# Fixed order on all DMA queues, a hand-pipelined first phase and weights paced in half tiles, in an attention and mixer kernel

## The chip, the cores and the metric

The kernel runs on one core of a Trainium2 chip. The metric is the device time of one execution in microseconds (us). Engines are named as in the profile: PE (TensorE: matmuls and weight loads), DVE (VectorE), ACT (ScalarE), POOL (GpSimd) and SP (SyncE, which here only issues DMAs). Each of SP and POOL has a queue of its own from which it issues DMAs in order.

## The reference

The input x has 2048 tokens of 1024 features, in bf16. Two branches read the normalised x. Branch A is attention over segments of 32 tokens with a memory of 8 rows that each segment hands to the next; branch B is a mixer with an MLP. Their sum and x make the output.

```python
# A: 32 heads of 128, 64 segments of 32 tokens
h = concatenate([mem, xs])                  # 8 memory rows + 32 tokens
q, k, v = h @ Wq, h @ Wk, h @ Wv
p = softmax(where(mask, q @ k.T * scale, -1e9))
o = (p @ v) @ Wo
mem = o[:8]                                 # for the next segment
out_A = o[8:]
# B
h = gelu(layernorm(x) @ w1)                 # 1024 -> 1024
hs = shifted quarters of h @ w2             # shifts of 1 and 2 tokens
x1 = x + hs
out_B = x1 + gelu(layernorm(x1) @ w3) @ w4  # 1024 -> 3584 -> 1024
```

## The kernel before

The serial chain of memories is not followed. The kernel computes, with sums over each segment, what the memories are if softmax is close to uniform over a segment ("speculative" units), runs the attention of all segments in parallel with them, and at the end compares the memories it got with those it assumed. A fallback that goes segment by segment stands behind a condition and isn't run here.

The order of PE's instructions is the order of the program text (`manual_schedule` with PE alone, line 186). On DVE, ACT, POOL and SP a scheduler chooses the order. Every engine takes its own instructions strictly in its order, so an instruction that waits holds up all behind it.

The stages, one after another on PE:

1. *First phase* (L202 to L301). Sixteen tiles of 128 tokens. For each, `norm` takes statistics on DVE (L222 to L227), two inverse square roots on POOL (L229), minus mean times root on DVE (nm2, L231), the branch-B normalisation `xn2` on ACT (L233), the branch-A normalisation `xn` on DVE (L237), and stores `xn` to a scratch in DRAM by POOL's queue (L238). For tiles 0 to 3 `xn2` is transposed by PE (L247), for tiles 4 to 15 by a DMA transpose on SP (L235). `stage1` multiplies by w1 (L264) and applies gelu (L266); `seg_sums` (L256) makes the sums over segments. Groups have 1, 1, 2, 2, 2, 4 and 4 tiles. w2 comes as one load of 2 MB (L298). w3's seven loads of 1 MB (L335) stand later in the text, but the scheduler lets them run in this phase.
2. *The w2 phase* (L306 to L329). For each tile the w2 matmuls (L315), the reload of `xn` from the scratch (L308), an add on DVE (L316) and statistics (L317), the root on POOL (L323), nm3 on DVE (L325), `xn3` on ACT (L327), the store of x1 (R1) by POOL's queue (L328) and a DMA transpose to `xn3T` on SP (L329).
3. *The MLP* (L432 to L466), four blocks of 512 tokens. A block has 28 groups of w3 matmuls (L436) with gelu (L437), and then for each of its four tiles loads of R1 and x (L453, L455), an add on POOL (L456), 56 w4 matmuls (L460), adds on DVE (L461) and the store of R (L466). Between them run 24 speculative units. Each loads 1 MB of Wv or Wo by SP (L364, L376, L398) into a pool of four weight slots and later multiplies it by a few columns (L370, L384, L404). `spec_step` runs one unit and loads the next. In the last block sixteen DMA transposes make `xT` from the scratch.
4. *The V phase* (L472 to L490). Eight loads of Wv (L475), 1024 matmuls (L481), evictions on ACT and DVE, stores of V (L486).
5. *Attention* (L607 to L671), five groups of tokens, eight groups of four heads in each. A group of heads loads 1 MB of Wq and of Wk (L629, L630) and its V (L524), and projects (L540). Scores of a tile (L551) go through DVE (L553), ACT's exp (L555), and DVE again (L557, L559, L563) to `Pn`, which a DMA transpose on SP (L566) turns into `PT` for the output matmuls (L575). `tick` places scores and outputs between projections by a clock estimated in the program; outputs come LAT = 8 estimated us after their scores. Wo comes in four loads of 2 MB in the first group (L637). At the third group of heads `block_setup` makes the transposed tokens of the next group, `hTb`, with four DMA transposes (L515) and four small DVE copies (L516). After a group its output matmuls (L593) run, with a load of R (L596), an add (L601) and the store of the result (L602) at the last of eight pieces.
6. *The end*: the comparison of the memories and the last output pieces.

Of the kernel before, what the change touches and what calls it, by code (L numbers as in the profile page):

```python
# [15 lines left out]
BF16 = mybir.dt.bfloat16  # L16
# [7 lines left out]
P = 128  # L24
# [6 lines left out]
H = 32  # L31
# [46 lines left out]
def kernel(  # L78
# [107 lines left out]
    with tc.manual_schedule(engines={mybir.EngineType.PE}), ExitStack() as actx:  # L186
# [5 lines left out]
        with ExitStack() as bctx:  # L192
            psum = bctx.enter_context(tc.tile_pool(name="psum", bufs=2, space=PSUM))
            with ExitStack() as hctx:
# [4 lines left out]
                nc.gpsimd.memset(hTB[:, :, 0:2], 0.0)  # L199
                nc.gpsimd.memset(hTB[:, :, S + 2:S + 4], 0.0)  # L200

                with ExitStack() as p0:  # L202
# [3 lines left out]
                    xts = [ring.tile([P, D], BF16, tag="xt", bufs=8, name=f"xt{n}") for n in range(NT)]  # L206

                    def load_x(n):
                        nc.sync.dma_start(xts[n][:], x_v[:, n, :])
# [5 lines left out]
                    for n in range(3, 8):  # L215
                        load_x(n)

                    def norm(n, xn2T, jj, on_pe):
                        xt = xts[n]
                        st = ring.tile([P, 2, 6], F32, tag="st")  # L220
                        for c in range(2):
                            nc.vector.bn_stats(st[:, c, :], xt[:, c * 512:(c + 1) * 512])  # L222
                        mv = ring.tile([P, 2], F32, tag="mv")
                        nc.vector.bn_aggr(mv[:], st[:])
                        ab = ring.tile([P, 2], F32, tag="ab")
                        nc.vector.tensor_scalar(ab[:, 0:1], mv[:, 1:2], EPS, None, op0=ALU.add)
                        nc.vector.tensor_scalar(ab[:, 1:2], ab[:, 0:1], EPS, mv[:, 1:2], op0=ALU.mult, op1=ALU.add)  # L227
                        rr = ring.tile([P, 2], F32, tag="rr")
                        nc.gpsimd.tensor_tensor(rr[:], ab[:], neghalf[:], op=ALU.pow)  # L229
                        nm2 = ring.tile([P, 1], F32, tag="nm2")  # L230
                        nc.vector.tensor_scalar(nm2[:], mv[:, 0:1], rr[:, 1:2], -1.0, op0=ALU.mult, op1=ALU.mult)  # L231
                        xn2 = ring.tile([P, D], BF16, tag="xn2")
                        nc.scalar.activation(xn2[:], xt[:], ACTF.Identity, bias=nm2[:], scale=rr[:, 1:2])  # L233
                        if not on_pe:
                            nc.sync.dma_start_transpose(xn2T[:, jj], xn2[:])  # L235
                        xn = ring.tile([P, D], BF16, tag="xn")
                        nc.vector.tensor_scalar(xn[:], xt[:], mv[:, 0:1], rr[:, 0:1], op0=ALU.subtract, op1=ALU.mult)  # L237
                        nc.gpsimd.dma_start(xn_v[:, n, :], xn[:])  # L238
                        if n + 8 < NT:
                            load_x(n + 8)  # L240
                        return xn, xn2

                    def transposes(xn2, xn2T, jj):
                        for k0 in (0, 4):
                            ps = psum0.tile([P, 4, P], F32, tag="tr")
                            for k in range(4):
                                nc.tensor.matmul(ps[:, k, :], xn2[:, (k0 + k) * P:(k0 + k + 1) * P], ident[:], start=True, stop=True)  # L247
                            if k0 == 0:
                                nc.vector.tensor_copy(xn2T[:, jj, k0:k0 + 4, :], ps[:])
                            else:  # L250
                                nc.scalar.copy(xn2T[:, jj, k0:k0 + 4, :], ps[:])

                    def seg_sums(n, xn):
# [3 lines left out]
                        nc.vector.tensor_copy(xsum[:, :, 4 * n:4 * n + 4], ps[:])  # L257

                    def stage1(n0, nt, xn2T, between):
                        w = nt * P  # L260
                        for co in range(KT):
# [5 lines left out]
                            if between and co % 2 == 1:  # L267
                                between.pop(0)()

                    groups = []  # L270
                    n0 = 0
                    for nt in (1, 1, 2, 2, 2, 4, 4):
                        groups.append((n0, nt))
                        n0 += nt
                    todo = []
                    prev = None
                    for (n0, nt) in groups:
                        xn2T = ring.tile([P, 4, KT, P], BF16, tag="xn2T", bufs=2)
                        on_pe = n0 < 4
                        trs, sms = [], []  # L280
                        for jj in range(nt):
                            xn, xn2 = norm(n0 + jj, xn2T, jj, on_pe)
                            if on_pe:
                                trs.append(lambda xn2=xn2, jj=jj, xn2T=xn2T: transposes(xn2, xn2T, jj))
                            sms.append(lambda n=n0 + jj, xn=xn: seg_sums(n, xn))
                        if prev is None:
                            for f in trs:
                                f()
                            todo = sms
                        else:  # L290
                            todo = trs + todo
                            stage1(*prev, todo)
                            for f in todo:
                                f()
                            todo = sms
                        prev = (n0, nt, xn2T)
                        if n0 == 4:
                            nc.sync.dma_start(w2_sb[:], w2_v)  # L298
# [554 lines left out]
```

## Time and profile before

| | |
|---|---|
| median of 3 runs | 1609.46 us (1600.1 to 1611.64) |
| the profiled execution | 1606.37 us |
| its span | 1604.6 us |
| mean granted PE clock | 0.988 |
| PE busy | 1537.0 us (96%) |
| DVE, ACT, POOL busy | 525.3, 511.5, 89.7 us |
| read from and written to DRAM | 191.52 and 42.53 MB |

The profile is of one execution. Its own time is 1.8 us more than the span, which runs from the first instruction to the last event. PE is busy nearly all the time, so time is to be found where PE waits. A wait on another engine counts only if PE, or the end of the program, comes to wait for it.

### The profile page before, as it was taken

The page shows a single profiled execution, that of the slowest core. Times are in us where ns is not written, and L with a number is a line of the kernel's source. Part 1 is how long each engine was busy: PE and PEld are TensorE (multiplying, and loading weights), DVE is VectorE, ACT ScalarE, POOL GpSimd, SP SyncE. Part 2 cuts the span into 40 slices and gives each one's busy share as a digit, 9 for nine tenths or more (in the row PEclk, how much of TensorE's full clock was granted, in tenths as well). Part 3 has the DMA queues.
Part 4 walks back from the last instruction along what each step waited for, and adds up shares of the span by engine and source line. Part 5 has one row for each costly group of instructions (what it writes and reads, how often), then busy time and mean ns, then how long its engine had stood idle before and what let it go on. Part 6 is the DMA issues. An engine that isn't in the chain of part 4 may idle for free.

```text
span 1604.6 us, 25081 instructions
## 1 busy us (share of the span) xinstructions
PE 1537.0 (96%) x10222; PEld 830.5 (52%) x10222; DVE 525.3 (33%) x1149; ACT 511.5 (32%) x1183; POOL 89.7 (6%) x114
## 2 busy tenths in 40 slices
PE   5799998999999999999999999999999999999998
PEld 4544444454454444444455645654655566466654
DVE  6248000001010112212235533551554165325541
ACT  4423300301202101111146623650563266146630
POOL 4223001001011010000000000000000000000000
PEclk9899999999999999999999999999999999999999
DMA  9869525265382567433369965993798388348521
GB/s 316 242 190 298 190 86 177 79 208 186 91 243 75 109 193 266 132 105 120 105 196 254 236 155 131 245 232 89 213 233 201 108 223 228 91 128 196 115 48 48
DMA packets 340087, 271.93 MB, mean 169 GB/s; under 512 B 155987, under 2 KB 309736, under 8 KB 339968
## 3 DMA queue, kind: packets, MB, share of 16 engines
q1 hardware_dynamic: 333888, 249.23, 58.2%
q0 software_dynamic: 6080, 21.05, 3.5%
q8 instruction: 82, 1.34, 0.4%
q14 instruction: 37, 0.30, 0.1%
HBM read 191.52 MB, written 42.53 MB: 146 GB/s over the span
## 4 chain that ended last, share of the span: by engine, by line
PE 73%; DMA 9%; DVE 1%; issue 1%; ACT 0%; POOL 0%; SPq 0%; ACTq 0%; POOLq 0%
PE ps L540 23%; PE pso L593 14%; PE ps L481 14%; PE ps L436 9%; PE ps L460 8%; DMA PT<-Pn_6360 3%; PE psO L575 2%; PE psS L551 2%; DMA PT<-Pn_6361 2%; DMA PT<-Pn_6359 1%; DMA hTb<-xn_scratch 1%; PE ps L693 1%; DMA R_scratch<-R_3128 1%; PE ps L404 1%; DMA wot<-in_A_Wo_dram 1%
## 5 line engine op out<-in xcount | busy, mean ns | idle before, releaser
L540 PE MATMUL ps<-hTb,wt 128*128 128x396 bf16 (+1 forms) x2560 | 403.7, 311 | 0.0
L540 PEld LDWEIGHTS <-wt 128*128 128x128 bf16 x3072 | 272.0, 98 | 167.3 <-issue 4.5
L481 PE MATMUL ps<-wt,xT 128*128 128x512 bf16 x1024 | 221.2, 379 | 0.0
L460 PE MATMUL ps<-w_sb,h3T 128*128 128x512 bf16 x896 | 198.5, 382 | 0.0
L437 ACT ACTIVATE h3T<-ps 128x512 bf16<-128x512 f32 x112 | 66.6, 597 | 315.0 <-PE ps L436 310.6
L481 PEld LDWEIGHTS <-xT 128*128 128x128 bf16 x1024 | 100.2, 98 | 120.8
L436 PEld LDWEIGHTS <-w_sb 128*128 128x128 bf16 x896 | 88.1, 99 | 112.3 <-issue 11.4
L460 PEld LDWEIGHTS <-h3T 128*128 128x128 bf16 x896 | 87.1, 98 | 103.3 <-issue 2.7
L557 DVE TENSOR_REDUCE sums<-sm 99x4 f32<-99x396 f32 (+1 forms) x176 | 97.6, 554 | 117.6 <-ACT sm L555 117.5
L553 DVE TENSOR_TENSOR sm<-psS,c_mask_reg_sb 99x396 f32<-99x396 f32 x160 | 91.2, 570 | 109.6 <-PE psS L551 108.9
L483 ACT CAST Vs<-ps 128x512 bf16<-128x512 f32 x64 | 37.4, 586 | 230.2 <-PE ps L481 177.5
L555 ACT ACTIVATE sm<-sm 99x396 f32<-99x396 f32 (+1 forms) x176 | 92.8, 527 | 54.0 <-DVE sm L553 49.8
L485 DVE CAST Vs<-ps 128x512 bf16<-128x512 f32 x64 | 44.3, 692 | 176.5 <-PE ps L481 172.7
L540 PE MATMUL ps<-hTb_5138,wt 128*128 128x403 bf16 x512 | 93.6, 335 | 2.4 <-ACT QT_6369 L544 1.5
L264 PE MATMUL ps<-xn2T,w_sb 128*128 128x256 bf16 (+2 forms) x448 | 65.9, 309 | 13.8 <-DMA xn2T<-xn_788 8.2
L601 DVE TENSOR_TENSOR ot<-pso,Rt 128x512 bf16<-128x512 f32 x32 | 22.1, 691 | 156.1 <-PE pso L593 152.8
L264 PEld LDWEIGHTS <-w_sb 128*128 128x128 bf16 x448 | 41.0, 106 | 32.7 <-issue 9.8
L436 PE MATMUL ps<-xn3T_1209,w_sb 128*128 128x512 bf16 x224 | 51.4, 393 | 4.8 <-ACT h3T L437 4.8
L315 PE MATMUL ps<-w_sb,hTB 128*128 128x512 bf16 x256 | 55.4, 379 | 0.0
L436 PE MATMUL ps<-xn3T_1210,w_sb 128*128 128x512 bf16 x224 | 51.0, 390 | 0.0
L436 PE MATMUL ps<-xn3T_1211,w_sb 128*128 128x512 bf16 x224 | 49.0, 379 | 0.0
L436 PE MATMUL ps<-xn3T_1212,w_sb 128*128 128x512 bf16 x224 | 48.5, 379 | 0.0
(613 smaller groups left out, 1407.1 us busy)
## 6 DMA issues: line engine op xcount, KB each, us to landing
wt<-in_A_Wq_dram SPq DMA_DIRECT2D x40, 1024.0 KB
wt<-in_A_Wk_dram SPq DMA_DIRECT2D x40, 1024.0 KB
wt<-in_A_Wv_dram SPq DMA_DIRECT2D x24, 1024.0 KB
w_sb<-in_B_w_dram SPq DMA_DIRECT2D x16, 1024.0 KB
V_scratch<-Vs SPq DMA_DIRECT2D x32, 512.0 KB
wot<-in_A_Wo_dram SPq DMA_DIRECT2D x8, 1024.0 KB
wo_sb<-in_A_Wo_dram SPq DMA_DIRECT2D x4, 2048.0 KB
Rt<-R_scratch SPq DMA_DIRECT2D x32, 256.0 KB
```

The costliest lines, as they stand in the source:

```text
L264: nc.tensor.matmul(ps[:, :w].rearrange("p (n t) -> p n t", t=P), w1_sb[:, k, co * P:(co + 1) * P], xn2T[:, :nt, k, :], start=(k == 0), sto ...
L315: nc.tensor.matmul(ps[:], hTB[:, k, o:o + P], w2_sb[:, k, ch * 512:(ch + 1) * 512], start=(k == 0), stop=(k == KT - 1))
L436: nc.tensor.matmul(ps[:].rearrange("p (n t) -> p n t", t=P), w3_sb[:, k, f * P:(f + 1) * P], xn3T[tb][:, :, k, :], start=(k == 0), stop=(k ...
L437: nc.scalar.activation(h3T[:, f, :], ps[:], ACTF.Gelu_apprx_tanh)
L460: nc.tensor.matmul(ps[:], h3T[:, f, j * P:(j + 1) * P], w4_sb[:, f, ch * 512:(ch + 1) * 512], start=(f == 0), stop=(f == FT - 1))
L481: nc.tensor.matmul(ps[:], xT[:, m4 * 4 + j, k, :], wv[:, k, :], start=(k == 0), stop=(k == KT - 1))
L485: nc.vector.tensor_copy(Vs[:, j, :], ps[:])
L540: nc.tensor.matmul(ps[:, :nb] if B["b"] in (0, 5) else ps[:, :nb].rearrange("p (t c) -> p t c", t=4), w[:, k, hh * P:(hh + 1) * P], B["rhs ...
L553: nc.vector.tensor_tensor(sm[:T, :, :T], S3, t["mask"][:].unsqueeze(1).to_broadcast((T, 4, T)), op=ALU.add)
L555: nc.scalar.activation(e[:T, :, :T], sm[:T, :, :T], ACTF.Exp, scale=LN2)
L557: nc.vector.tensor_reduce(ss, e[:T, :, :T], axis=AX.X, op=ALU.add)
L593: nc.tensor.matmul(self.ps[:], self.oX[:, h, self.gl * P:(self.gl + 1) * P], wo_sb[:, h, self.cc], start=(h == 0), stop=(h == H - 1))
```

## The change

The order of the text now holds on SP and POOL as well, in all stages, and in the first phase also on DVE and ACT. The text is rearranged to suit.

- *First phase.* Groups are 1, 1 and then pairs. Statistics, normalisations, transposes and sums are written between the matmuls of the group before. Tiles 0 to 7 are normalised for branch B on DVE and transposed by PE; tiles 8 to 15 stay with ACT and the DMA transpose. nm2 is made by POOL, and the sums are copied by ACT. x has six buffers instead of eight. w2 comes in four loads of 512 KB, w3 in fourteen of 512 KB from tile 10 on and through the w2 phase.
- *xn kept.* The branch-A normalisation stays in SBUF (`xn_keep`, three of the weight slots and one tile more) and isn't reloaded in the w2 phase. nm3 is made by POOL. The DMA transpose stands ahead of the R1 store in the text.
- *MLP.* The speculative weights are loaded by POOL's queue. The first load stands right after the first block's w3 matmuls; a step comes once per tile of the w4 part and after every seventh w3 group, one ahead in the first two blocks and two ahead after. The sixteen `xT` transposes stand four to a tile.
- *V phase.* Wv is loaded two ahead by POOL's queue. The four loads of Wo move here. The first Wq and Wk are loaded at its seventh group.
- *Attention.* Wq and Wk of the next group of heads are loaded in halves of 512 KB, one at each `tick`, and then V. A tick places at most one scores item and one outputs item, and scores only if fewer than five wait for their output. LAT is 10. `block_setup` is at the same place in the text. R is loaded at the first of the eight pieces, and it and the result go by POOL's queue.

At the program's start DVE's order changes. Before, xt_113, xt_114 and xt_115 are the x tiles 0, 1 and 2, and nm_150 is nm2 of tile 0:

```order
L222 BN_STATS st<-xt_113 128x6 x2
L224 BN_AGGR mv<-st 128x2
L226 TENSOR_SCALAR ab<-mv 128x1
L227 TENSOR_SCALAR ab<-ab,mv 128x1
L222 BN_STATS st<-xt_114 128x6 x2
L224 BN_AGGR mv<-st 128x2
L226 TENSOR_SCALAR ab<-mv 128x1
L227 TENSOR_SCALAR ab<-ab,mv 128x1
L222 BN_STATS st<-xt_115 128x6
L231 TENSOR_SCALAR nm_150<-mv,rr 128x1
L237 TENSOR_SCALAR xn<-xt_113,mv,rr 128x1024
```

The same place after, where xt_121 and xt_124 are the x tiles 0 and 1, and xn_147 is tile 0 normalised for branch B:

```order
L244 BN_STATS st_135<-xt_121 128x6
L247 BN_STATS st_135<-xt_121 128x6
L248 BN_AGGR mv_136<-st_135 128x2
L249 TENSOR_SCALAR ab_137<-mv_136 128x1
L250 TENSOR_SCALAR ab_137<-ab_137,mv_136 128x1
L259 TENSOR_SCALAR xn_147<-xt_121,mv_136,rr_138 128x1024
L244 BN_STATS st_149<-xt_124 128x6
L282 CAST xn2T<-ps 128x512
```

The normalisation of tile 0 has moved ahead of the statistics of tiles 1 and 2, and is made by DVE itself.

On SP in the MLP before, the loads of R (R_2992, R_3128), of x (xt) and of the speculative weights (wt) stand in one line:

```order
L455 DMA xt<-in_A_x_dram 128x1024
L364 DMA wt<-in_A_Wv_dram 128x8x512
L453 DMA R_2992<-R_scratch 128x1024
L455 DMA xt<-in_A_x_dram 128x1024
L364 DMA wt<-in_A_Wv_dram 128x8x512 x2
L453 DMA R_3128<-R_scratch 128x1024
```

After, the weights stand on POOL, in the first block of the MLP as follows, between the adds (L521) and the stores (L534) of R:

```order
L418 DMA wt<-in_A_Wv_dram 128x8x512
L521 TENSOR_TENSOR R_2327<-R_2327,xt 128x1024
L534 DMA R_scratch<-R_2327 128x1024
L521 TENSOR_TENSOR R_2393<-R_2393,xt 128x1024
L418 DMA wt<-in_A_Wv_dram 128x8x512
L534 DMA R_scratch<-R_2393 128x1024
```

The weight loads have left SP's line of R and x loads and joined POOL's line of adds and stores.

On SP in the first group of attention before, the `hTb` transposes of the next group stood apart, between the transposes of Pn and the whole weights:

```order
L630 DMA wt<-in_A_Wk_dram 128x8x512
L566 DMA_TRANSPOSE PT<-Pn_6359 128x4x112
L515 DMA_TRANSPOSE hTb<-xn_scratch 128x8x112
L566 DMA_TRANSPOSE PT<-Pn_6360 128x4x112
L515 DMA_TRANSPOSE hTb<-xn_scratch 128x8x112 x2
L629 DMA wt<-in_A_Wq_dram 128x8x512
L566 DMA_TRANSPOSE PT<-Pn_6361 128x4x112
```

After, at the third group of heads of the first group:

```order
L642 DMA_TRANSPOSE PT<-Pn_5144 128x4x112
L642 DMA_TRANSPOSE PT<-Pn_5142 128x4x112
L591 DMA_TRANSPOSE hTb<-xn_scratch 128x8x112 x4
L697 DMA wt<-in_A_Wq_dram 128x4x512
L642 DMA_TRANSPOSE PT<-Pn_5143 128x4x112
L697 DMA wt<-in_A_Wq_dram 128x4x512
L697 DMA wt<-in_A_Wk_dram 128x4x512
L642 DMA_TRANSPOSE PT<-Pn_5144 128x4x112
L697 DMA wt<-in_A_Wk_dram 128x4x512
```

The four `hTb` transposes have moved together and earlier, and the weights come as halves between the transposes of Pn.

The core of the diff:

```diff
-    with tc.manual_schedule(engines={mybir.EngineType.PE}), ExitStack() as actx:
+    with tc.manual_schedule(engines={mybir.EngineType.PE, mybir.EngineType.SP, mybir.EngineType.Pool}), ExitStack() as actx:
...
+            def load_w3():
+                c, k0 = w3_at[0] // 2, 4 * (w3_at[0] % 2)
+                w3_at[0] += 1
+                if c < 7:
+                    nc.sync.dma_start(w3_sb[:, k0:k0 + 4, c * 512:(c + 1) * 512], w3_v[:, k0:k0 + 4, c * 512:(c + 1) * 512])
...
+                xn_keep = [wpool.tile([P, 4, D], BF16, tag="w", name=f"xnk{i}") for i in range(3)] + [keep.tile([P, 4, D], BF16, name="xnk3")]
+
+                with tc.manual_schedule(engines={mybir.EngineType.DVE, mybir.EngineType.Activation}), ExitStack() as p0:
...
+                    NPE = 8
...
+                            if n >= NPE:
+                                nc.gpsimd.tensor_scalar(nm2[:], mv[:, 0:1], rr[:, 1:2], -1.0, op0=ALU.mult, op1=ALU.mult)
+
+                    def norm2(n, xn2T, jj):
+                        st, mv, ab, rr, nm2 = stats[n]
                         xn2 = ring.tile([P, D], BF16, tag="xn2")
+                        if n < NPE:
+                            nc.vector.tensor_scalar(xn2[:], xts[n][:], mv[:, 0:1], rr[:, 1:2], op0=ALU.subtract, op1=ALU.mult)
+                        else:
+                            nc.scalar.activation(xn2[:], xts[n][:], ACTF.Identity, bias=nm2[:], scale=rr[:, 1:2])
                             nc.sync.dma_start_transpose(xn2T[:, jj], xn2[:])
+                        return xn2
+
+                    def norm1(n):
+                        st, mv, ab, rr, nm2 = stats[n]
+                        xn = xn_keep[n // 4][:, n % 4]
+                        nc.vector.tensor_scalar(xn, xts[n][:], mv[:, 0:1], rr[:, 0:1], op0=ALU.subtract, op1=ALU.mult)
+                        nc.gpsimd.dma_start(xn_v[:, n, :], xn)
+                        load_x(n + 6)
+                        if n < 4:
+                            nc.sync.dma_start(w2_sb[:, 2 * n:2 * n + 2, :], w2_v[:, 2 * n:2 * n + 2, :])
+                        elif n >= 10:
+                            load_w3()
+                        return xn
...
+                            def prep(i, m0=m0, nxt=nxt, box=box):
+                                box[i] = norm2(m0 + i, nxt, i)
+                                norm_stats(m0 + 2 + i)
+                                xns[m0 + i] = norm1(m0 + i)
...
+                            prep(0)
+                            between[1] = lambda: (tr(0, 0), prep(1))
+                            between[2] = lambda: tr(0, 1)
+                            between[5] = lambda: tr(1, 0)
+                            between[6] = lambda: tr(1, 1)
+                        between[3] = lambda n0=n0: sums_of(n0 - 1)
+                        between[4] = lambda n0=n0: sums_of(n0 - 2)
+                        stage1(n0, nt, cur, between)
...
-                        xn = ring.tile([P, D], BF16, tag="xn")
-                        nc.sync.dma_start(xn[:], xn_v[:, n, :])
...
-                        nc.vector.tensor_scalar(nm3[:], mv[:, 0:1], r3[:], -1.0, op0=ALU.mult, op1=ALU.mult)
+                        nc.gpsimd.tensor_scalar(nm3[:], mv[:, 0:1], r3[:], -1.0, op0=ALU.mult, op1=ALU.mult)
...
+                        nc.sync.dma_start_transpose(xn3T[n // 4][:, n % 4], xn3[:])
                         nc.gpsimd.dma_start(R1_v[:, n, :], x1[:])
-                        nc.sync.dma_start_transpose(xn3T[n // 4][:, n % 4], xn3[:])
...
+                        load_w3()
...
-                    nc.sync.dma_start(wv[:], Wv_v[:, :, hg * 512:(hg + 1) * 512])
+                    nc.gpsimd.dma_start(wv[:], Wv_v[:, :, hg * 512:(hg + 1) * 512])
...
-                def spec_load():
-                    if units:
+                def spec_load(depth=1):
+                    while units and len(pending) < depth:
...
                 for tb in range(4):
+                    depth = 1 if tb < 2 else 2
...
+                        elif n > 0:
+                            spec_step(depth)
...
+                if 1 <= hg < 5:
+                    nc.gpsimd.dma_start(wo_sb[:, (hg - 1) * 8:hg * 8, :], Wo_v[:, (hg - 1) * 8:hg * 8, :])
...
+                if hg == (6 if self.late else 0):
+                    self.Rt = iop.tile([P, 512], F32, tag="Rt")
+                    nc.gpsimd.dma_start(self.Rt[:], R_v[:, self.gi, self.cc])
...
+                    nc.gpsimd.dma_start(out_v[:, self.gi, self.cc], ot[:])
...
+                for k0 in (0, 4):
+                    loads.append(lambda w=w, src=src, k0=k0: nc.sync.dma_start(w[:, k0:k0 + 4, :], src[:, k0:k0 + 4, cs_]))
...
+            turn[0] += 1
+            if turn[0] % every == 0:
+                load_some(1)
+            done = set()
+            for item in list(smalls):
+                due, kind, fn = item
+                if due <= clock[0] and kind != blocked and kind[0] not in done and not (kind[0] == "S" and flying[0] >= 5):
...
-        LAT = 8.0
+        LAT = 10.0
```

256 lines of the change are left out of this document (140 added, 116 removed).

## The prediction

> **What bounds the kernel now.** I read the page's busy shares first, then the engines by stage, then the waits of TensorE. The columns of the stage rows are the stretch, its length, busy time with instruction count of PE, PE's weight loads, DVE, ACT and POOL, then granted clock, DMA share and GB/s.
>
> ```profile
> PE 1537.0 (96%) x10222; PEld 830.5 (52%) x10222; DVE 525.3 (33%) x1149; ACT 511.5 (32%) x1183; POOL 89.7 (6%) x114
> ...
> 0.00:96.41 96.41, 69.20 (x608) 47.96 (x609) 40.85 (x133) 43.12 (x77) 26.07 (x45) 0.93 0.82 241
> ...
> 151.70:587.70 436.00, 422.42 (x2572) 204.07 (x2571) 41.05 (x87) 69.20 (x115) 41.30 (x35) 0.98 0.50 148
> 587.70:809.00 221.30, 221.02 (x1025) 100.00 (x1022) 44.79 (x66) 37.41 (x64) 2.16 (x5) 1.00 0.45 150
> 809.00:1555.00 746.00, 724.91 (x5340) 428.59 (x5340) 343.44 (x747) 343.58 (x911) 0.00 (x0) 1.00 0.72 177
> ```
>
> PE is busy 1537.0 of a 1604.6 us span, and no other engine passes 33%. So an edit can win only PE's 67.6 us of idle time and what a reduced clock stretches. The idle time lies 27.2 us in the first phase (96.41 − 69.20), 13.6 in the MLP, 0.3 in the V phase and 21.1 in attention. The waits of PE (total, times, longest) say for whom:
>
> ```profile
> PE ps L247 <- ACT xn_152 L233: 13.4, 1, 13.4
> PE psO L575 <- DMA PT<-Pn_6360: 10.1, 9, 2.1
> PE ps L264 <- DMA xn2T<-xn_788: 8.2, 1, 8.2
> PE ps L370 <- DMA wt<-in_A_Wv_dram: 5.2, 2, 3.9
> PE ps L436 <- ACT h3T L437: 4.8, 1, 4.8
> PE ps L264 <- DMA xn2T<-xn_474: 3.6, 1, 3.6
> PE gps_3027 L384 <- DMA wot<-in_A_Wo_dram: 3.5, 2, 3.0
> PE psO L575 <- ACT oT_m L578: 2.9, 5, 0.7
> PE psO L575 <- DMA PT<-Pn_6359: 2.6, 3, 1.2
> PE psO L575 <- DMA PT<-Pn_6361: 2.5, 4, 1.5
> ```
>
> No row is a large one; the change works on each of them. PE's instructions stay the same but for four more tiles transposed on it.
>
> **The change part by part: the start.**
>
> ```profile
> 1.23 0.71 POOL L121 DMA_DIRECT2D c_ident_sb<-c_ident  x1 [0.77 <-POOLq L834]
> ...
> 5.56 0.73 POOL L229 TENSOR_TENSOR rr<-ab,neghalf 128x2 f32<-128x2 f32 x1
> ...
> 7.63 1.29 DVE L222 BATCH_NORM_STATS2 st<-xt_114 128x6 f32<-128x512 bf16 x2 [2.16 <-DMA xt_114<-in_A_x_dram]
> ...
> 11.97 0.54 DVE L237 TENSOR_SCALAR xn<-xt_113,mv,rr 128x1024 bf16<-128x1024 bf16 x1
> 12.09 1.24 ACT L233 ACTIVATE xn_152<-xt_113,nm_150,rr 128x1024 bf16<-128x1024 bf16 x1 [7.25 <-DVE nm_150 L231]
> ...
> 16.24 1.86 PE L264 MATMUL ps<-xn2T,w_sb 128*128 128x128 bf16 x16 [1.82 <-DVE xn2T L249]
> ```
>
> ```profile
> c_ident_sb<-c_ident POOLq DMA_DIRECT2D x1, 32.0 KB, 5.7
> ```
>
> The inverse roots of tile 0 were ready at 5.56 + 0.73 = 6.29, but ACT's normalisation waited until 12.09 for nm_150, which stood in DVE's order behind statistics of two later tiles whose data had not arrived. Now DVE normalises tile 0 at once: 6.29 + 0.54 = 6.83. The identity lands at 1.23 + 5.7 = 6.93. So PE starts at about 7.0 instead of 13.4. Before, 2.84 us passed from there to the first w1 matmul (16.24). DVE's copy of one half now stands behind one statistic of x tile 1, from 7.63 with half of 1.29, so it ends near 9.0. The w1 matmuls then begin at 9.0 (at 9.8 with the old 2.84): **−7.2**.
>
> **The rest of the first phase.**
>
> ```profile
> 25.61 0.69 PE L247 MATMUL ps<-c_ident_sb,xn_322 128*128 128x128 bf16 x8
> ...
> 39.25 3.52 PE L264 MATMUL ps<-xn2T,w_sb 128*128 128x256 bf16 x16 [3.57 <-DMA xn2T<-xn_474]
> ...
> 42.81 1.91 PE L264 MATMUL ps<-xn2T,w_sb 128*128 128x256 bf16 x16
> ...
> 64.03 6.50 PE L264 MATMUL ps<-xn2T,w_sb 128*128 128x512 bf16 x16 [8.23 <-DMA xn2T<-xn_788]
> ...
> 70.57 3.61 PE L264 MATMUL ps<-xn2T,w_sb 128*128 128x512 bf16 x16
> ```
>
> From 16.24 to 96.41 are 80.2 us. Of these 3.57 + 8.23 = 11.8 are waits for DMA transposes, and the sixteen matmuls behind each wait took 3.52 and 6.50 instead of 1.91 and 3.61, 4.5 us more. The Trainium skill ("TensorE: Matmul & The Clock Gate") has the clock halved when the array idles; 3.52 against 1.91 agrees. Without waits and slow matmuls 63.9 stay. Four more tiles on PE cost 4 × 0.69 = 2.8, the last segment sums 0.5.
>
> Tiles 8 to 15 still go by DMA transpose, now in pairs. A pair's 64 matmuls take 4 × 1.91, about 7.5 us. The second tile of the next pair is normalised on ACT once a quarter of the group is done (1.9 + 0.25 + 1.24, so 3.4 into it), and then transposed:
>
> ```profile
> 28.36 2.10 SPq L235 DMA_TRANSPOSE xn2T<-xn_455  x1
> ...
> 36.93 1.24 ACT L233 ACTIVATE xn_614<-xt_120,nm_612,rr 128x1024 bf16<-128x1024 bf16 x1 [4.52 <-DMA xn2T<-xn_455]
> ...
> 158.52 1.23 SPq L329 DMA_TRANSPOSE xn3T_1212<-xn_1820  x1
> 162.93 2.06 ACT L437 ACTIVATE h3T<-ps 128x512 bf16<-128x512 f32 x4 [4.43 <-DMA xn3T_1212<-xn_1820]
> ```
>
> Such a transpose took 8.6 us (28.36 to 36.93) under the full load of the first phase and 4.4 (158.52 to 162.93) in quiet. It lands 7.8 to 12 us into the group, so each of four pairs stalls 0.3 to 4.5 us. I take 1 each, nearer the quiet row, because w3 now comes in half pieces between them: 4.0. That makes 9.0 + 63.9 + 2.8 + 0.5 + 4.0 = 80.2 for the end of the phase, against 96.4: **−16** with the start, from −19 (no stall) to −10 (2.5 each).
>
> **Into the MLP.** TensorE leaves the w2 phase at 151.7, with DVE behind it:
>
> ```profile
> 154.43 0.67 DVE L316 TENSOR_TENSOR x_1788<-ps,xn 128x512 f32<-128x512 f32 x1
> ```
>
> ```profile
> R_scratch<-x_1256 POOLq DMA_DIRECT2D x1, 512.0 KB, 4.1
> ...
> R_scratch<-x_1674 POOLq DMA_DIRECT2D x1, 512.0 KB, 8.7
> ```
>
> The last add began 2.8 us after PE's end, and the transpose landed 11.3 after it (162.93), which left the wait of 4.8. Without the reload of xn and with nm3 on POOL, DVE has less to do per tile than PE and keeps up, so the transpose lands about 8.7 after PE's end and the wait falls to 2.3. But h3T takes over memory that the R1 store reads, and that store now stands behind the root and nm3 on POOL: issued 3.0 after PE's end, landed 4.1 to 8.7 later, 7.1 to 11.7 after it. At 11.7 the wait would be 5.3, nothing gained. I take −2.5 and, of the 1.6 to 2.9 us by which slow matmuls followed the two waits above, another −1.5: **−4**, from −5 to +1.
>
> **The speculative weight loads.**
>
> ```profile
> 259.77 7.98 SPq L364 DMA_DIRECT2D wt<-in_A_Wv_dram  x2
> ...
> 265.24 2.10 PE L370 MATMUL ps<-xb,wt 128*128 128x71 bf16 x32 [3.88 <-DMA wt<-in_A_Wv_dram]
> ```
>
> PE waited 5.2 + 3.5 = 8.7 us for Wv and Wo. One load was issued at 259.77, and PE wanted it at 261.4. In SP's order it stood behind an R load and an x load that wait for buffers, not for bandwidth. Now each 1 MB load is issued from POOL a step ahead: 7 blocks of 8 matmuls at 3.61/16 each make 12.6 us, 56 w4 matmuls as much. What is queued behind it on POOL are R stores and the next add, which nothing needs within 6 us. How long 1 MB takes by that queue no row shows; 512 KB took 4.1 to 8.7, so 1 MB lies between 5 and 17. I take 9, nearer to the quick rows, since this stage has a DMA share of 0.50. Then the waits go, and with the two longest (3.9 and 3.0) about 2.2 each of slow matmuls: **−13**, at most −14.5. The Trainium skill ("DMA: Bandwidth & Descriptors", Issuing engines are not separate DMA queues) says that initiating on another engine saves only the sequencer's time; by it this term would be 0. The rows above speak of a position in SP's order, which does move.
>
> **V phase.** 8 MB of Wo move into it. PE never waits there, and the DMA share is 0.45: **0**. The cover is 27 us of matmuls per group of heads; without it the price is that of the speculative loads.
>
> **Attention.**
>
> ```profile
> 828.48 1.22 SPq L566 DMA_TRANSPOSE PT<-Pn_6359  x1
> ...
> 832.62 0.35 PE L575 MATMUL psO<-PT,V_6371 106*128 106x106 bf16 x4
> ...
> 918.73 2.63 SPq L515 DMA_TRANSPOSE hTb<-xn_scratch  x2
> ```
>
> The waits for PT (10.1 + 2.6 + 2.5) and for oT_m (2.9) sum to 18.1, none over 2.1. A PT that is issued at 828.48 is used 4.1 later. The outputs now follow their scores 2 us later, only one of each kind runs per tick, and weight loads enter SP half a tile at a time: the waits should go. New is a knot in the first group of heads: four hTb transposes stand in a row in SP's order, ahead of a PT (4 × 1.3 = 5.3 us from 2.63 for two), and DVE's copies from them stand between softmax steps. Less the slack of 2, some 3 to 5 us of stall and 2 of slow matmuls: 7. In the later groups they fall beside the output matmuls, which need no PT. **−11**, from −18 to 0 (if the gain is eaten by this knot and by transposes as late as before).
>
> **The end.** The output store moves to POOL:
>
> ```profile
> 1599.95 0.33 SPq L602 DMA_DIRECT2D out_dram<-ot  x1
> ```
>
> It took until 1604.6, 4.7 us; a small POOL load took 5.7: **+1** (0 to 2).
>
> **The rivals.** *Transposes as late as before.* Each pair stalls 4.5 and loses 1.6 of clock (4 × 6.1 against the 4.0 taken, so +20), and attention gains nothing (+11): 1566 + 31 = 1597. For it: the share of DMA in the first phase is 0.82, and the w3 pieces still precede transposes. Against: fewer bytes move there, since the reload of xn and the 2 MB block of w2 are gone.
>
> *POOL's queue is too slow: slower than before.* Eleven of the speculative loads (three in the first block of tokens, eight in the second) have one step of 12.6 us and no more. At 17 us, twice 8.7, each stalls 4.4 and loses 1.6 of clock: 11 × 6 = 66, and the 13 won are lost: 1566 + 79 = 1645. The other gains are 30, so it decides from 11 × (x − 12.6) = 30, an x of 15.3 us. For it: the row of 8.7. Against: 4.1 for the same size, and little other traffic.
>
> *The queue does not matter.* The speculative waits stay, by the rule named above: 1566 + 13 = 1579. Against it stands the issue at 259.77.
>
> *The knot is worse*, each of five groups paying 7: 28 more, 1594. Against: in the later groups the order has output matmuls there.
>
> **How the numbers follow.** −16 − 4 − 13 + 0 − 11 + 1 = −43 on the profiled run's own 1606.4 gives 1563. The median of the runs shown is 1609.5, 3.1 above that run, so I predict **1566**. Within 1% of the median (1593 to 1626) counts as no change. Chances: the forecast 0.67, late transposes 0.12, the queue does not matter 0.08, the knot 0.06, POOL too slow 0.07. The terms at their best are −19 − 5 − 14.5 − 18 = −56.5, 1553; the runs spread by 9 below their median, so the low end is 1546. At their worst short of a rival, −10 + 1 − 8 − 0 + 2 = −15, 1594; with late transposes in reach the high end is 1597. Faster 0.84: the forecast, the queue, and half of late transposes and of the knot; same 0.09; slower 0.07.
>
> **What would show it.** Right: the first w1 matmul at 9 to 10; the first w2 matmul near 80; no PE wait on Wv or Wo; PT waits under 5 us in all, most of it in the first group; PE busy again near 1535. Wrong: PE waits on speculative tiles of several us each, POOL loads landing after 13 us or more, waits for xn2T in each pair above 2.5, or PT waits spread over all groups.

## The result, and the profile after

The changed kernel takes 1561.55 us (median of 4 runs, 1556.14 to 1570.57), the kernel before beside it 1606.32 us. The ratio is 0.9728, 95% interval 0.9667 to 0.9790. The profiled execution is the longest of the four, 1570.57 us with a span of 1568.8. Of all executions that follow one stands apart: it is one of the six of run e11, at a granted clock of 0.557 and 2675.56 us, and is not counted in that run's ratio.

The page's busy shares of the changed kernel:

```profile
PE 1524.0 (97%) x10382; PEld 842.2 (54%) x10382; DVE 527.1 (34%) x1106; ACT 513.9 (33%) x1218; POOL 162.8 (10%) x238
```

Its engines by stage, with the columns of the prediction's rows:

```profile
0.00:82.14 82.14, 67.83 (x768) 60.47 (x769) 40.58 (x107) 44.82 (x112) 29.99 (x53) 0.98 0.74 220
82.14:137.39 55.25, 55.25 (x262) 25.06 (x259) 46.20 (x90) 15.07 (x13) 19.71 (x43) 1.00 0.96 233
137.39:159.38 21.99, 7.07 (x33) 3.14 (x32) 3.27 (x7) 5.60 (x6) 2.53 (x7) 0.76 1.09 179
159.38:567.10 407.72, 407.71 (x2539) 198.43 (x2538) 36.88 (x68) 65.90 (x111) 62.39 (x57) 1.00 0.46 146
567.10:789.60 222.50, 221.31 (x1025) 100.09 (x1023) 44.78 (x65) 37.41 (x64) 13.79 (x16) 1.00 0.48 160
789.60:1520.00 730.40, 723.82 (x5359) 431.75 (x5359) 346.49 (x753) 345.08 (x913) 26.88 (x50) 1.00 0.74 184
```

The waits of PE:

```profile
PE ps L498 <- ACT h3T L499: 14.9, 1, 14.9
PE ps L280 <- DVE xn_147 L259: 7.2, 1, 7.2
PE psO L651 <- DMA PT<-Pn_5143: 3.0, 2, 2.6
PE ps L297 <- DMA xn2T<-xn_940: 2.9, 1, 2.9
PE ps L616 <- DMA wt<-in_A_Wq_dram: 1.9, 2, 1.4
PE ps L280 <- DVE xn_302 L259: 1.5, 1, 1.5
PE ps L556 <- ACT Vs L558: 1.2, 1, 1.2
```

All rows of this view sum to 36.8 us, before to 61.0. In the MLP proper (159.38 to 567.10) PE is busy 407.71 of 407.72 us; no wait on Wv or Wo is left. In attention one place with a wait of over 1 us is left. But one wait is longer than any that the change removed: 14.9 us at the entry into the MLP, where before it was 4.8.

The stages by PE's first instructions of each, against the sum of the prediction. The third column is a second execution of the same kernel (the run e9 below):

| from, to | before, us | changed, us | changed again, us | predicted difference | found |
|---|---|---|---|---|---|
| start to first w2 matmul | 96.41 | 82.14 | 79.91 | −16 | −14.3, −16.5 |
| w2 phase | 55.25 | 55.25 | 55.25 | 0 | 0 |
| first w3 matmul to the first after the wait for h3T | 11.92 | 21.99 | 9.96 | −4 | +10.1, −2.0 |
| the rest of the MLP | 423.97 | 407.72 | 406.24 | −13 | −16.3, −17.7 |
| V phase | 222.05 | 223.40 | 222.41 | 0 | +1.4, +0.4 |
| attention to the first matmul of the comparison | 752.55 | 733.44 | 738.39 | −11 | −19.1, −14.2 |
| from there to the span's end | 42.45 | 44.86 | 44.84 | +1 | +2.4, +2.4 |
| span | 1604.6 | 1568.8 | 1557.0 | −43 | −35.8, −47.6 |

The entry into the MLP in the profile of the changed kernel, in order of time:

```profile
124.91 8.46 SPq L387 DMA_TRANSPOSE xn3T_1413<-xn_1746  x1
...
139.82 0.69 DVE L375 TENSOR_TENSOR x_1966<-ps,xnk_111 128x512 f32<-128x512 f32 x1 [3.06 <-DMA R_scratch<-x_1822]
...
143.88 0.26 POOL L384 TENSOR_SCALAR nm_1996<-mv,r_1994 128x1 f32<-128x1 f32 x1
...
144.13 1.24 ACT L386 ACTIVATE xn_1890<-x_1858,nm_1888,r_1886 128x1024 bf16<-128x1024 f32 x1 [9.57 <-DMA xn3T_1413<-xn_1746]
...
154.59 1.24 ACT L386 ACTIVATE xn_1998<-x_1966,nm_1996,r_1994 128x1024 bf16<-128x1024 f32 x1 [2.41 <-DMA xn3T_1413<-xn_1854]
155.85 1.23 SPq L387 DMA_TRANSPOSE xn3T_1414<-xn_1998  x1
...
158.74 1.58 ACT L499 ACTIVATE h3T<-ps 128x512 bf16<-128x512 f32 x3 [2.91 <-DMA xn3T_1414<-xn_1998]
159.38 1.01 PE L498 MATMUL ps<-xn3T_1411,w_sb 128*128 128x512 bf16 x2 [14.93 <-ACT h3T L499]
```

Two things run late here. DVE's adds for the last two tiles wait 0.92 and 3.06 us for R1 stores to free their buffers. And the transposes are slow: a single one holds SP's queue 8.46 us, and the last is issued at 155.85, 18 us after the w2 phase. The second is what PE waits for. nm3 of the last tile (nm_1996) is ready at 144.14, but ACT makes the tile's xn3 (xn_1998) only at 154.59. xn3 has four buffers, and ACT cannot write one again before the transpose that reads it has landed: xn_1746's transpose, issued at 124.91, frees its buffer for xn_1890 at 144.13, 19.2 us later, and so on down to xn_1854's.

How full the DMA engines are shows in the view by stretches of ten us (the DMA share, a busy share that can come out above 1, is the last column but one), and then in the time from issue to landing of the first and of a late R1 store (512 KB):

```profile
80.00:90.00 10.00, 9.63 (x66) 5.18 (x65) 5.15 (x10) 2.26 (x6) 1.39 (x3) 1.00 0.01 4
...
112.00:122.00 10.00, 10.00 (x48) 4.53 (x47) 8.95 (x17) 3.72 (x3) 4.12 (x9) 1.00 1.15 263
...
142.00:152.00 10.00, 2.46 (x12) 1.00 (x11) 0.92 (x3) 3.54 (x3) 1.37 (x3) 0.84 1.24 162
```

```profile
R_scratch<-x_1418 POOLq DMA_DIRECT2D x1, 512.0 KB, 3.2
...
R_scratch<-x_1930 POOLq DMA_DIRECT2D x1, 512.0 KB, 13.1
```

Just ahead of the w2 phase's transposes the DMA engines stand still (share 0.01). From 92 to 152 us their share is 1.07 and more, and a store that took 3.2 us at first takes 13.1.

### The profile page after: what moved, and what is told of

It reads as the page before. It is cut to its first block, busy times and chain, and to the rows that moved or that the text cites. A ratio compares the mean times of both kernels' runs of the same rounds, so it can differ in the third digit from the quotient of the medians.

```text
span 1568.8 us, 25432 instructions
## 1 busy us (share of the span) xinstructions
PE 1524.0 (97%) x10382; PEld 842.2 (54%) x10382; DVE 527.1 (34%) x1106; ACT 513.9 (33%) x1218; POOL 162.8 (10%) x238
## 3 DMA queue, kind: packets, MB, share of 16 engines
q1 hardware_dynamic: 286208, 189.46, 47.6%
## 5 line engine op out<-in xcount | busy, mean ns | idle before, releaser
L616 PE MATMUL ps<-hTb,wt 128*128 128x396 bf16 (+1 forms) x2560 | 419.2, 310 | 0.0
L616 PEld LDWEIGHTS <-wt 128*128 128x128 bf16 x3072 | 265.5, 98 | 151.3 <-DMA wt<-in_A_Wq_dram 2.7
L498 PEld LDWEIGHTS <-w_sb 128*128 128x128 bf16 x896 | 87.2, 98 | 118.8 <-issue 17.1
L616 PE MATMUL ps<-hTb_5320,wt 128*128 128x403 bf16 x512 | 98.7, 338 | 2.8 <-DMA wt<-in_A_Wq_dram 1.9
L677 POOL DMA_DIRECT2D out_dram<-ot x32 | 17.4, 545 | 593.2 <-DVE ot L676 480.2
L297 PE MATMUL ps<-xn2T,w_sb 128*128 128x256 bf16 (+1 forms) x576 | 64.5, 270 | 5.1 <-DMA xn2T<-xn_940 2.9
L498 PE MATMUL ps<-xn3T_1411,w_sb 128*128 128x512 bf16 x224 | 50.3, 387 | 14.9 <-ACT h3T L499 14.9
L297 PEld LDWEIGHTS <-w_sb 128*128 128x128 bf16 x576 | 52.0, 102 | 11.6 <-issue 6.2
L498 PE MATMUL ps<-xn3T_1414,w_sb 128*128 128x512 bf16 x224 | 49.0, 379 | 0.0
L498 PE MATMUL ps<-xn3T_1413,w_sb 128*128 128x512 bf16 x224 | 49.0, 379 | 0.0
```

The source lines that it names most:

```text
L297: nc.tensor.matmul(ps[:, :w].rearrange("p (n t) -> p n t", t=P), w1_sb[:, k, co * P:(co + 1) * P], xn2T[:, :nt, k, :], start=(k == 0), sto ...
L498: nc.tensor.matmul(ps[:].rearrange("p (n t) -> p n t", t=P), w3_sb[:, k, f * P:(f + 1) * P], xn3T[tb][:, :, k, :], start=(k == 0), stop=(k ...
L616: nc.tensor.matmul(ps[:, :nb] if B["b"] in (0, 5) else ps[:, :nb].rearrange("p (t c) -> p t c", t=4), w[:, k, hh * P:(hh + 1) * P], B["rhs ...
```

## The experiments

**w3 out of the w2 phase (e1).** Is it the eight w3 half pieces, 4 MB, that the change put into the w2 phase?

```diff
+                    while w3_at[0] < 14:
+                        load_w3()
                     for n in range(NT):
                         sums_of(n)
...
                         nc.gpsimd.dma_start(R1_v[:, n, :], x1[:])
-                        load_w3()
```

> The changed kernel with one thing altered: the eight w3 half pieces that it loads during the w2 phase are issued right after the last x tile of the first phase, where its DMA share was 0.01 to 0.53. Theory (4 MB of w3 on top of the R1 stores and the DMA transposes fill the DMA engines in the w2 phase, share 1.07 to 1.24, so that the last transposes and stores land late): the wait of TensorE at the entry into the MLP falls from 14.9 to 2 to 5 us, and the time by 10 to 14 us, to about 1549. Rival (the R1 store is late because it stands behind root and nm3 on POOL): the wait stays above 10 and the time within 3 us of the changed kernel.

It took 1558.38 us, ratio to before 0.9690 (0.9650 to 0.9729). The wait, from the waits of PE:

```profile
PE ps L499 <- ACT h3T L500: 1.0, 1, 1.0
```

The wait is nearly gone with the pieces, although the R1 store still stands behind root and nm3 on POOL. The rival falls. In e1 the DMA share over the w2 phase is 0.81, against 0.96 in the changed kernel, and the R1 stores land sooner:

```profile
R_scratch<-x POOLq DMA_DIRECT2D x16, 512.0 KB, 3.2
```

In the kernel before the share over this phase was 1.05. The change takes 4 MB out of the phase with the reloads of xn, and puts 4 MB of w3 in. e1 moves the bytes and also takes the eight issues out of SP's line, where they stood between the transposes for 0.6 to 1.1 us each; the two were not taken apart. The time fell by less than expected, because 14.9 us was not what this wait usually is:

**The changed kernel again (e5, e9).** Nothing is altered in either.

> The changed kernel again, nothing altered. In the profile of the run with LAT 8 the wait at the entry into the MLP was 1.2 us, in that with the weight loads on SP 5.0, in that of the changed kernel 14.9, with the same loads in the w2 phase in all three. Theory (the DMA engines are at their limit there, so that the length of this wait differs from one execution to the next): it comes out other than 14.9, below 10, and the time between 1553 and 1565. Rival (the 14.9 belongs to this order): it comes out within 3 us of 14.9 and the time near 1570.

> The changed kernel, nothing altered, beside the three that follow on one chip, so that differences of a few us can be read. The theory that its wait at the entry into the MLP differs between executions expects a third value for it, anywhere from 1 to 15 us, and a spread of its times of 10 us or more.

They took 1568.24 us (1559.70 to 1578.14; above what was expected; ratio to before 0.9767, 0.9706 to 0.9827) and 1562.66 us (1558.85 to 1578.68). The wait at the entry was 8.3 in the first and 2.9 in the second:

```profile
PE ps L498 <- ACT h3T L499: 8.3, 1, 8.3
```

```profile
PE ps L498 <- ACT h3T L499: 2.9, 1, 2.9
```

With 5.0 (e2) and 1.2 (e3), that makes five profiles of the same w2 phase with waits of 14.9, 8.3, 5.0, 2.9 and 1.2. The length differs from one execution to the next. That it does so because the DMA engines are at their limit is argued from the shares, and a full share alone doesn't do it: in the kernel before, at 1.05, the wait was 4.8, 5.7 (e4) and 5.3 us (e6). What is shown is that it is 1.0 in every profile (e1, e7, e8, e10, e11, e12) in which the 4 MB are loaded earlier.

> The kernel with w3 all loaded in the first phase, again. Theory (the w3 pieces in the w2 phase cost time): a wait of 1 us at the entry into the MLP for the fourth time, and a time 4 to 10 us under that of the control. Rival (what isn't lost there is lost elsewhere): within 3 us of the control.

On one chip with e9, w3 early took 1558.64 us (1554.54 to 1560.37) against 1562.66: 4.0 us less, and 6 us of spread where the control has 20. Ratios to before are 0.9697 (0.9666 to 0.9729) and 0.9745 (0.9702 to 0.9789); the intervals overlap, so the 4 us are likely, not certain.

**The speculative loads: the queue or the place in it (e2, e4).** In e2 the changed kernel issues them from SP, at the same place in its text; in e4 the kernel before issues them from POOL, where its scheduler puts them.

```diff
# e2: the changed kernel, for all three kinds of unit
-                    nc.gpsimd.dma_start(wv[:], Wv_v[:, :, hg * 512:(hg + 1) * 512])
+                    nc.sync.dma_start(wv[:], Wv_v[:, :, hg * 512:(hg + 1) * 512])
# e4: the kernel before, for all three
-                    nc.sync.dma_start(wv[:], Wv_v[:, :, hg * 512:(hg + 1) * 512])
+                    nc.gpsimd.dma_start(wv[:], Wv_v[:, :, hg * 512:(hg + 1) * 512])
```

> The changed kernel with the 24 speculative weight loads issued by SP again, at the same place in the text. Theory (it is the position in a queue that matters, and the text order is as good on SP): waits of TensorE for these weights stay under 3 us in all, and the time within 1% of the changed kernel, 1550 to 1575. Rival (POOL's queue is what won it): 5 to 9 us of waits return, with slow matmuls behind them, and the time rises by 8 to 14 us.

> The kernel before with one thing altered: the speculative weight loads go by POOL's queue, where the scheduler puts them between the adds and stores of R. Theory (SP's order held them up): the 8.7 us of waits for these weights fall to under 3, and the time by 8 to 13 us, to 1594 to 1600. Rival (the issuing queue doesn't matter): the waits stay near 8.7 and the time within 3 us of the kernel before.

e2 took 1567.60 us (1563.60 to 1570.74; ratio to before 0.9746, 0.9706 to 0.9787), and no wait for speculative weights stands among PE's waits. The MLP after its entry took 407.9 us, as with POOL's queue (407.7). So POOL's queue is not what won it. What is left is the text: the place of the loads in a line and how many steps ahead they are issued. The two were not taken apart.

e4 took 1603.91 us, ratio 0.9975 (0.9953 to 0.9997): 6 us less than the kernel before in the same session, less than the 8 to 13 expected. The rest of the MLP took 414.5 us, 9.5 less than before. The waits for Wo went, but those for Wv did not (4.4 us in all):

```profile
241.10 2.12 POOL L456 TENSOR_TENSOR R<-R,xt 128x1024 f32<-128x1024 f32 x1 [7.10 <-DMA R<-R_scratch]
243.17 0.94 POOL L364 DMA_DIRECT2D wt<-in_A_Wv_dram  x1
...
249.63 1.78 PE L370 MATMUL ps<-xb,wt 128*128 128x71 bf16 x32 [4.03 <-DMA wt<-in_A_Wv_dram]
```

On POOL the load stands behind an add that waits 7.10 us for R. Once issued, at 243.17, it lands within 6.5 us. The load was held up in another line, in the same way as on SP. So neither expectation holds as it stands: another queue helps as far as its order happens to be better, and where the order is written the queue makes no difference to this stage.

**LAT (e3, e6).** The number alone, 10 to 8 in the changed kernel and 8 to 10 in the kernel before.

```diff
# e3: the changed kernel
-        LAT = 10.0
+        LAT = 8.0
# e6: the kernel before
-        LAT = 8.0
+        LAT = 10.0
```

> The changed kernel with LAT 8 instead of 10. Theory of the prediction (the two us of slack take the waits for PT away): the waits for PT rise from 3.8 us in all to 10 or more, spread over the groups, and the time by 5 to 12 us. Rival (the half tiles and the lighter DMA load in the first group do it): the waits stay under 7 us and the time within 4 us of the changed kernel.

> The kernel before with LAT 10 instead of 8 and nothing else. Theory (two more us between scores and outputs are what takes the waits for PT away, as the prediction had it): the waits for PT and oT_m fall from 18.1 us to under 5, and the time by 10 to 20 us. Rival (it is the order on SP and the half tiles that make the attention stage shorter; the larger LAT only repays what these cost): the waits stay above 10 and the time within 6 us of the kernel before.

e3 took 1591.25 us, ratio to before 0.9903 (0.9866 to 0.9940), some 30 us more than the changed kernel; e6 took 1593.75 us, 0.9913 (0.9879 to 0.9948), 13 us less than the kernel before. PE's waits for PT, of e3 and then of e6:

```profile
PE psO L651 <- DMA PT<-Pn: 28.4, 25, 3.5
```

```profile
PE psO L575 <- DMA PT<-Pn: 3.0, 4, 1.2
```

The attention stage, as in the table, took 765.0 us in e3 and 739.3 in e6, against 752.6 before and 733.4 and 738.4 changed. So the number alone wins 13 of the 14 to 19 us. In e6 the waits for PT and oT_m are 5.9 us in all (3.0 and 2.9), a little above the 5 expected. At LAT 8 the new order is 12 us slower in this stage than the old one: it needs the larger LAT, and with it gives little more than LAT alone (in e5 and e2, with LAT 10, the stage took 737.3 and 740.6). A larger LAT than 10 on the old order, and one item of each kind per tick by itself, were not run. Of e3 the theory expected 5 to 12 us; it is the direction that was right, the size far off.

**Half tiles or whole ones (e11).** With w3 early, as in e10:

```diff
-                for k0 in (0, 4):
-                    loads.append(lambda w=w, src=src, k0=k0: nc.sync.dma_start(w[:, k0:k0 + 4, :], src[:, k0:k0 + 4, cs_]))
+                loads.append(lambda w=w, src=src: nc.sync.dma_start(w[:], src[:, :, cs_]))
```

> The same, with Wq and Wk loaded whole, 1 MB each in one issue, instead of in halves. Theory (LAT does the work, the half tiles little): waits for PT and the time within 4 us of the run with halves. Rival (half tiles keep PT's transposes from standing behind a whole load): waits for PT rise by 10 us or more and the time by 8 or more.

It took 1568.84 us, ratio 0.9761 (0.9727 to 0.9795), against 1558.64 for e10 on the same chip. Waits for PT in e11 and in e10:

```profile
PE psO L652 <- DMA PT<-Pn: 14.4, 13, 4.2
```

```profile
PE psO L652 <- DMA PT<-Pn: 7.2, 5, 2.8
```

The theory that half tiles do little falls: 7 us of waits go with them, and the attention stage took 745.9 us in e11 against 737.8 in e10. The other 2 of the 10 us lie in the first phase (84.3 against 82.2), which this edit doesn't touch and which took 79.5 to 84.3 us in the profiles of the new order. Whether half tiles would gain anything in the old order was not run.

**The knot in the first group (e7, e8).** In the profile of the changed kernel, the four hTb transposes, what follows them on SP, and what PE waits for:

```profile
818.58 6.10 SPq L591 DMA_TRANSPOSE hTb<-xn_scratch  x4
824.78 0.54 SPq L697 DMA_DIRECT2D wt<-in_A_Wq_dram  x1
825.44 1.19 SPq L642 DMA_TRANSPOSE PT<-Pn_5143  x1
```

```profile
829.46 0.35 PE L651 MATMUL psO<-PT,V_6548 106*128 106x106 bf16 x4 [2.60 <-DMA PT<-Pn_5143]
831.85 1.52 PE L616 MATMUL ps<-hTb_5320,wt 128*128 128x403 bf16 x4 [1.35 <-DMA wt<-in_A_Wq_dram]
```

In e7 each of four groups of heads gets one of them, with w3 early; e8 is e7 with LAT 12.

```diff
+        parts = []
...
-                    nc.sync.dma_start_transpose(hTb[:, i], xn_d[a:a + 112, :])
-                    nc.vector.tensor_copy(hTb[:, i, :, 96:99], MZ[:, :, t["r0"]:t["r0"] + 3])
+                    def part(i=i, a=a, t=t, hTb=hTb):
+                        nc.sync.dma_start_transpose(hTb[:, i], xn_d[a:a + 112, :])
+                        nc.vector.tensor_copy(hTb[:, i, :, 96:99], MZ[:, :, t["r0"]:t["r0"] + 3])
+                    parts.append(part)
...
+                if parts:
+                    parts.pop(0)()
```

> The changed kernel with w3 all loaded in the first phase (as in the run on that), and the four hTb transposes of the next group issued one in each of four groups of heads instead of four in a row. Theory (the knot: four transposes ahead of a PT in SP's order): the waits for PT and Wq in the first group of attention at its third group of heads, 4.0 to 4.9 us in all profiles of the new order, go below 1, and the time is 3 to 7 us under that of the run with w3 early (1558), so about 1553. Rival (DMA load of the first groups): they stay above 3.

> The same kernel with LAT 12. Theory (the waits for PT left over, 1 to 3 us here and there, are single late transposes, and two more us cover them): waits for PT under 2 us in all, the time 2 to 6 us under that of the run with the spread transposes alone. Rival (with only five PT buffers more distance holds up the next scores): no gain, or 3 us and more lost.

e7 took 1564.29 us, ratio 0.9728 (0.9695 to 0.9762), where about 1553 was expected; e8 1563.17 us, 0.9742 (0.9703 to 0.9780), 1.1 under e7 where 2 to 6 were expected. The wait at the third group of heads did go below 1 (0.4 for Wq, none for PT), as the theory of the knot has it. But twelve waits for PT, 13.0 us in all, stand in e7's profile against five of 9.1 us in e1's; five of the twelve are in the first group of tokens, where e1 has one. Spreading moved the cost instead of removing it: the attention stage took 748.9 us, against 738.5 in e1. In e8 LAT 12 leaves 0.7 us of waits for PT, and 8.5 us in nine waits for Wq. Its first half now stands behind a transpose in four groups of heads of each group of tokens but the last; that this is what delays it is not shown. Neither came out faster than e1 (1558.38, in another session).

**LAT 12 without the spread (e12).** e10 with this one number:

```diff
-        LAT = 10.0
+        LAT = 12.0
```

> The same with halves and with LAT 12. Theory (single late transposes are left): waits for PT fall from 9.1 us to under 2, and the time by 4 to 9 us against the run with LAT 10, to 1550 or so. Rival (five PT buffers): no gain, within 2 us.

It took 1554.98 us (1552.16 to 1556.29), ratio 0.9671 (0.9641 to 0.9702), 3.7 us under e10 and 7.7 under the changed kernel (e9) in the same session. Waits for PT, and what has taken their place:

```profile
PE ps L617 <- DMA wt<-in_A_Wq_dram: 5.7, 2, 3.3
...
PE psO L652 <- DMA PT<-Pn: 0.8, 1, 0.8
```

PT hardly makes PE wait any more: 6.4 us of these waits are gone, but those for Wq grew by 4.3. All its six times are under the lowest of e9, and no other version that was run has a lower median; against e10 the times and the intervals overlap.

## Why the prediction was right, and where not

The sum said 1566 and the kernel takes 1561.55. The total fits better than its terms, and that is luck: the gains in the MLP and in attention came out larger than predicted, and one term, in the profiled execution, with the other sign. By the table, the entry into the MLP was 14 us worse there than its term, the speculative loads 3 and attention 8 us better. In e9 the entry was 2 us worse, the two others 5 and 3 better.

*The start and the first phase: right.* PE's first rows in the changed kernel's timeline:

```profile
7.18 1.03 PE L280 MATMUL ps<-c_ident_sb,xn_147 128*128 128x128 bf16 x8 [7.18 <-DVE xn_147 L259]
8.46 3.87 PE L297 MATMUL ps<-xn2T,w_sb 128*128 128x128 bf16 x32 [0.25 <-ACT xn2T L284]
```

No run takes this phase apart; what follows is read from the traces. PE started at 7.18, released by DVE's normalisation as predicted (7.0), and the first w1 matmul came at 8.46 (9.0). The first w2 matmul came at 82.14, and at 79.91 in e9, predicted 80.2. The waits of the four DMA-transposed pairs were 0.84, 2.94, none and 0.92, 4.7 in all against 4.0 taken. The term's best end doesn't follow from its own numbers: without any stall it is 16.2 + 4.0, so −20 and not −19.

*Into the MLP: wrong, the step that failed.* The prediction took the wait from 4.8 to 2.3, with 5.3 as the worst. It was 14.9 in the profile, and over five profiles between 1.2 and 14.9, with two beyond the worst. The step that failed is the transpose. It was given 4.4 us, the quiet row, and no term had ACT wait for a buffer that an earlier transpose holds. In the profile four transposes took 12.6 to 19.2 us from issue to landing, and ACT waited for them in turn. That DVE "keeps up" held for DVE's own work, and failed by 4 us in its waits for R1 stores, but this was not what PE waited for: nm3 was ready 10 us before ACT could use it. In e5 ACT waited in the same way; in e9 and e2 its last normalisation came in time, and the last transpose landed 5.7 and 8.2 us after the start of it, against 4.2 in e1. The last R1 store, on which the prediction's worst case rests, was issued at 144.09 and took 10.2 us, so it landed ahead of the last transpose. The change moves eight w3 pieces into this phase, in place of the reloads of xn, with a share of 1.05 before. The prediction counted the reloads that go, and the pieces only in the first phase. The term should have carried the moved 4 MB with its new place, as e1 shows: out of there, 1.0. The bound of +1 was too near, and the mechanism that reached beyond it (slow transposes that hold ACT's buffers) was among the rivals only for the first phase and attention.

*The speculative loads: right, a little small.* Predicted −13, found −16.3 and −17.7 in the stage. 1 MB by POOL's queue landed in 7.0 us (median), against 9 taken from bounds of 5 to 17. Here is the row, of the changed kernel's DMA issues:

```profile
wt<-in_A_Wv_dram POOLq DMA_DIRECT2D x24, 1024.0 KB, 7.0
wot<-in_A_Wo_dram POOLq DMA_DIRECT2D x8, 1024.0 KB, 7.0
```

The rival of a slow queue, from 15.3 us on, was far off. The rival of a queue that doesn't matter has to be split. The rule of the Trainium skill ("DMA: Bandwidth & Descriptors", Issuing engines are not separate DMA queues), that another issuing engine saves only the time of issuing, agrees with e2, where SP serves as well as POOL: 407.9 us against 407.7. What the rival drew from it, that the waits would therefore stay, fails: they were the cost of a position in a line, and the same edit rewrote the line.

*The V phase: right.* +1.4 and +0.4 us with 8 MB of Wo moved into it.

*Attention: the sign right, the size small, the reason only half named.* Predicted −11, found −19.1 and −14.2. The prediction put LAT, one of each kind per tick and half tiles together as one cause. e6 and e3 take LAT out: alone it gives −13 on the old order, and the new order without it loses 12. The knot cost 4.0 us where 3 to 5 were predicted, and in the later groups of tokens the hTb transposes cost next to nothing, as predicted. The rival of a knot in all five groups falls; it also counted one too many, since the last group makes no hTb (the transposes stand at 818.6, 923.2, 1063.2 and 1203.0 us). The sign "PT waits under 5 us" came in the profile (3.8) but not in e5 (5.6) and e9 (8.6).

*The end: +2.4 against +1.* The last store, in the changed kernel's timeline:

```profile
1562.01 0.54 POOL L677 DMA_DIRECT2D out_dram<-ot  x1 [5.83 <-DVE ot L676]
```

From its issue to the end of the span (1568.8) are 6.8 us by POOL's queue; by SP's, in the kernel before, they were 4.7. The 5.7 of the prediction came from a load of 32 KB. But in e2 the same store goes by POOL's queue too, and there it took 4.7 us (from 1556.83 to 1561.5). So the queue alone doesn't explain the 2 us; their cause stays open.

The rival of transposes as late as before falls in the first phase and in attention; its mechanism struck in the phase between. The sign "PE busy again near 1535" did not come either: it is 1524.0. The terms had counted on fewer slow matmuls, and the sign had not.

## What to carry to other kernels

When a load is moved, add up the DMA of the stage into which it goes, and look for the stage next to it that stands still: here 4 MB went into a phase that runs at a share of 0.81 without them and of 0.96 with them (1.07 to 1.24 from its second ten us on), while the stretch just ahead of it was at 0.01. See also how many buffers the slower transfers hold, and who waits for these. If a load comes late, see in the queue's order what it stands behind before giving it another queue; a better place in the same queue did as well. When one edit changes an order and a distance in time together, try the distance on the old order first, since here one number gave 13 of the stage's 14 to 19 us.

## What the runs showed that was not expected

At a DMA share of 1.05 and more, from the second ten us of the w2 phase on, the same text waited 1.2, 2.9, 5.0, 8.3 and 14.9 us at one place in five executions; with 4 MB less in that phase the wait was 1.0 in six. The profile of one execution gave no sound size for such a wait, and this was the largest in it.

At LAT 8 the new order's waits for PT sum to 28.4 us, but its attention stage is 26.6 us longer than that of e9 with 8.6 us of such waits: 20 us more waiting and 7 us besides. In the same stretch PE is busy 734.0 us against 727.1, at a granted clock of 0.99 against 1.00, so the 7 are matmuls that took longer.
